# A recurrent-memory transformer on one core: the left rows' q and k of all segments made at once in step 0, against phase by phase in the steps

## The chip, the cores and the metric

The kernel runs on one core of one Trainium2 chip. The time is device time in microseconds (us) of one execution; what counts is the median over runs. The engines are PE (TensorE: PE for matmuls, PEld for its weight loads), DVE (VectorE), ACT (ScalarE), POOL (GpSimd) and SP (SyncE, which here only issues transfers). Transfers are moved by 16 DMA engines, whoever issues them.

## The reference

Two independent parts read the normalised input and are summed with it.

```
x = A_x                                   # [1, 2048, 1024], bf16
xn = layernorm(x)
out = x + A(xn) + B(xn)

A: mem = mem0                             # [8, 1024]
   for s in 64 segments of 32 rows:
       h = [mem ; xn of the segment]      # 40 rows
       q, k, v = h @ Wq, h @ Wk, h @ Wv   # 32 heads of 128, each W is 1024 x 4096
       p = softmax(mask(q k^T / sqrt(128)))   # memory rows see all rows; the others those up to their own
       o = (p v) @ Wo                     # 4096 x 1024
       mem = first 8 rows of o            # goes into the next segment
       out rows of the segment = the other 32

B: r = xn @ w_r; the two rows with the largest r go through a gated MLP (1024 -> 3584 -> 1024)
   and are added back, weighted by sigmoid(r)
```

The memory makes the 64 segments a chain: a segment can't begin before the one ahead has given its eight memory rows. Only what does not hang on the memory can be made ahead.

## The kernel before

**Steps.** One step is one segment. Its 40 rows are split: 32 "main" rows, the eight of memory and the first 24 of the segment, must be multiplied in the step. The last eight rows of the segment, the "left" rows, don't see the chain in their q, k and v; those of four segments are gathered to another block of 32 rows (a group G of four steps, j = 0 to 3 in it) and are multiplied one group ahead, in spare places of the steps.

**Weights.** Wq, Wk, Wv and Wo are 32 MB, cut in 64 granules of 512 KB, used in the same order in every step. 44 stay in SBUF after step 0 ("resident", tiles `wres`). 20 are "streamed": granule 6 is kept whole in PSUM (`KEPT`) and half of granule 25 too; the other 18.5 are fetched anew in every step from a packed copy in DRAM (`wsc`) into five slots (`wstream`, tiles `g`). `fetch` (L327) is issued by SP as soon as PE is done with the slot that is to be overwritten.

**A step.** It has six phases, `PHASES`, q and k of the first 16 heads, q and k of the others, then v in two halves. A phase p runs over eight granules, index kc: `PSm += ST[:, kc]^T W` (L669), four matmuls of 32 output rows side by side, with the 32 main rows as the stationary operand (`ST`) and 512 columns of weights moving. In phases where left rows are due, the same granule is used a second time with the left rows' `STL` (`left_pass`, L647). `left_of(s)` says which: in step j = 1 both q phases and in j = 2 both k phases for the next group, in j = 3 and j = 0 one v phase each; in step 0 all six for group 0. Between granules stand `hooks[p, kc]`: turning q and k (L516), scores (L534, L536), softmax, attention (L584, L586). Then 16 Wo granules, index w, add to `WO` (L730; the left rows' `WL` once in a group). The result's memory rows are written to `XN` (L791), whose end marks the end of a step, and turned into the next step's `ST`.

**Left q and k.** A left phase's PSUM (`PSl`) is copied to `XBl` (L695) and stored to DRAM in `ql_d` (L698), rows of a group by head columns. Each step loads its segment's share to `LX` (`new_lx`, L458, by POOL at w = 9 of the step before), turns it with four transposes at phase 1 kc 5 (`turn_lx`, L465) and copies it to `QKL` (L467), which scores read.

**Step 0** also loads the residents, x (`XP`, in the homes of late Wo granules, for the rows' statistics and B's router), makes the copies `wsc` (`copy_block`, 20 transfers by POOL), and spreads DVE's work over granules (`side`: statistics of 15 further tiles, `spread`, 16 `router_tile`). After step 63 the MLP of B follows, with its 22 MB of weights loaded into the homes that the last step leaves.

**Order.** The order on each engine and queue is written out by hand (`tc.manual_schedule()`): what is issued earlier in the program stands earlier in its engine's queue; semaphores for tiles' readers and writers are added to it.

Of the kernel before, what the change touches and what calls it, by code (L numbers as in the profile page):

```python
# [27 lines left out]
def kernel(  # L28
# [58 lines left out]

    def granule_out(t, g):
        return t[:, :] if g < 48 else t.rearrange("p (hh d) -> p hh d", hh=2)
# [14 lines left out]
    ql_d = [dram.tile([4, P, 512], BF16, name=f"ql_d{t}") for t in range(NT)]  # L104

# [14 lines left out]

    def load_resident(g):
        t = home(g, [P, 2048], BF16, f"wres{g}")
        nc.sync.dma_start(out=granule_out(t, g), in_=granule_dram(g))
        res_tiles[g] = t
# [52 lines left out]
    XP = {}  # L177

    def load_x(u):
        XP[u] = home(resident[-3 - u], [P, 2048], BF16, f"XP{u}")  # L180
        nc.sync.dma_start(out=XP[u].rearrange("p (a d) -> p a d", a=2),
                          in_=x2[2 * u * P:(2 * u + 2) * P, :].rearrange("(a p) d -> p a d", a=2))

    def xt(t):
        return XP[t // 2][:, (t % 2) * D:(t % 2 + 1) * D]

# [103 lines left out]
    def norm_left(t, G):  # L290
        mr = two_rows(ML[:, G, :], "ri")
        nc.vector.tensor_scalar(out=t[:, :], in0=t[:, :], scalar1=mr[:, 0:1], scalar2=mr[:, 1:2],
                                op0=ALU.subtract, op1=ALU.mult)

# [39 lines left out]
    def keep(g, t):  # L334
        for c, K in KEPT_COLS[g].items():
# [5 lines left out]
            nc.vector.tensor_copy(out=XK[:, :], in_=PTB)  # L341
# [29 lines left out]
    def fetch_moe():  # L371
        while moe and free_homes:
            what = moe.pop(0)
            h = free_homes.pop(0)
            t = home(h, [P, 2048], BF16, "MW") if h >= 0 else wstream.tile([P, 2048], BF16, tag="g", name="g")
# [16 lines left out]

    load_x(0)
    nc.sync.dma_start(out=WRB, in_=B_w_r.unsqueeze(0).to_broadcast([P, D]))
    load_seg(0)
    XL0 = load_left(0, one.tile([P, 256], BF16, tag="vl", name="XL0")[:, :])
# [4 lines left out]
    n_x = 1  # L401
    n_q = 0
    for g in range(48):
        if g in streamed:
            n_q += 1
            if n_q < N_SLOT:
                fetch()
            continue
        if n_q >= N_SLOT:
            break  # L410
        load_resident(g)
        if g % 2 == 1 and n_x < NT // 2:
            load_x(n_x)
            n_x += 1
    todo_res = [g for g in resident if g not in res_tiles]
# [6 lines left out]
    norm_left(XL0, 0)  # L422
    STL = new_stl(XL0)

    side = {}
    for t in range(1, NT):
        side[t] = lambda t=t: row_stats(xt(t), S6, MV[:, t, :])
    side[NT] = lambda: spread(1, NT)
    for t in range(NT):
        side[NT + 2 + t] = lambda t=t: router_tile(t)  # L430
    side[2 * NT + 2] = router_out
    side[2 * NT + 10] = router_top

    def after(s, g):

        if s == 0:
            if g in side:
                side[g]()
            if g % 2 == 1 and g >= 8 and to_copy:
                copy_block(to_copy.pop(0))  # L440
            if n_x_left and g % 2 == 1:
                load_x(n_x_left.pop(0))
            while todo_res and todo_res[0] <= g + 2 * 64 // n_str + 8 and (todo_res[0] < resident[-10] or g >= 2 * NT + 12):
                load_resident(todo_res.pop(0))
# [8 lines left out]
    n_x_left = list(range(n_x, NT // 2))  # L453

    def new_lx(s):
        t = lx[0] = one.tile([P, 512], BF16, tag="bA", name="LX")
        G, j = divmod(s, 4)
        nc.gpsimd.dma_start(out=t[:, :], in_=ql_d[G].rearrange("m (q s r) c -> (m q) s r c", q=4, s=4)[:, j])  # L458

    lx = [None]  # L460

    def turn_lx():
        PTq = PTB.rearrange("p (i c) -> p i c", i=4)
        for il in range(4):
# [463 lines left out]
```

## Time and profile before

| what | us |
|---|---|
| runs: median (lowest, highest) of 3 | 1919.79 (1911.71, 1925.86) |
| profiled execution: own time | 1914.95 |
| its span on the core | 1913.2 |
| end of step 0 (L791), end of step 63 | 129.9, 1852.2 |
| PE, DVE, ACT, POOL busy | 1607.9, 906.8, 703.0, 294.0 |

A row of a stretch of the span reads: start:end, length; busy us of PE, PEld, DVE, ACT and POOL with their instructions in brackets; the granted clock of PE (1.00 is full speed); the mean busy share of the 16 DMA engines; GB/s. A row of a group of instructions: line, engine, operation, out<-in, shapes, count | busy us, mean ns of one | idle time of the engine ahead of it and what ended that. A row of a wait: who waited (q: the engine's queue) <- for whom: us in all, times, longest. A row of transfers: out<-in, who issues, count, KB each, us from issue to landing. The mean of one matmul is its stay in the pipeline, some 380 ns; how fast they follow each other is read from busy time or from the chain, whose rows are start, us, what.

### The profile page before, as it was taken

The page shows a single profiled execution, that of the slowest core. Times are in us where ns is not written, and L with a number is a line of the kernel's source. Part 1 is how long each engine was busy: PE and PEld are TensorE (multiplying, and loading weights), DVE is VectorE, ACT ScalarE, POOL GpSimd, SP SyncE. Part 2 cuts the span into 40 slices and gives each one's busy share as a digit, 9 for nine tenths or more (in the row PEclk, how much of TensorE's full clock was granted, in tenths as well). Part 3 has the DMA queues.
Part 4 walks back from the last instruction along what each step waited for, and adds up shares of the span by engine and source line. Part 5 has one row for each costly group of instructions (what it writes and reads, how often), then busy time and mean ns, then how long its engine had stood idle before and what let it go on. Part 6 is the DMA issues. An engine that isn't in the chain of part 4 may idle for free. (4 is left out here: it accounts for less than half of the span.)

```text
span 1913.2 us, 82718 instructions
## 1 busy us (share of the span) xinstructions
PE 1607.9 (84%) x36320; PEld 891.0 (47%) x36320; DVE 906.8 (47%) x2884; ACT 703.0 (37%) x1886; POOL 294.0 (15%) x590
## 2 busy tenths in 40 slices
PE   3558898888889888989889898989888898889864
PEld 1224545444454445545454554545454544545443
DVE  6824544554455445444554454445444544455430
ACT  1113433443334343434344343334333443343320
POOL 2201111111110211112111111211121111111110
PEclk8669999999999999999999999999999999999995
DMA  9999999999999999999999999999999999999998
GB/s 369 399 363 378 358 381 365 380 379 354 383 352 390 350 382 376 378 381 369 387 353 373 370 372 362 362 387 365 370 363 384 376 366 385 365 386 368 393 390 330
DMA packets 224441, 712.39 MB, mean 372 GB/s; under 512 B 33664, under 2 KB 44464, under 8 KB 224080
## 3 DMA queue, kind: packets, MB, share of 16 engines
q1 hardware_dynamic: 194384, 671.18, 92.9%
q0 software_dynamic: 21056, 28.07, 4.4%
q10 hardware_dynamic: 8640, 7.87, 1.2%
q8 instruction: 283, 4.64, 0.9%
q14 instruction: 78, 0.64, 0.1%
HBM read 694.32 MB, written 22.29 MB: 375 GB/s over the span
## 5 line engine op out<-in xcount | busy, mean ns | idle before, releaser
L669 PE MATMUL PSm<-wres,ST 128*32 128x512 bf16 x8448 | 720.2, 385 | 21.2 <-DVE ST L283 6.7
L669 PEld LDWEIGHTS <-ST 128*32 128x32 bf16 x12288 | 325.8, 96 | 396.4 <-issue 166.9
L669 PE MATMUL PSm<-g,ST 128*32 128x512 bf16 x3588 | 362.4, 387 | 88.5 <-DMA g<-wsc 60.3
L685 ACT CAST XB<-PSm 128x512 bf16<-128x512 f32 x256 | 150.0, 586 | 306.9 <-PE PSm L669 305.3
L730 PEld LDWEIGHTS <-OT 128*32 128x32 bf16 x8192 | 214.1, 97 | 104.1 <-issue 80.8
L730 PE MATMUL WO<-wres,OT 128*32 128x256 bf16 x5632 | 237.2, 275 | 14.0 <-issue 8.9
L647 PE MATMUL PSl<-wres,STL 128*32 128x512 bf16 x2112 | 200.3, 390 | 1.5 <-issue 1.4
L526 DVE COPY KT<-BT 128x512 bf16<-128x512 bf16 x128 | 52.5, 410 | 307.7 <-ACT XB L685 148.9
L458 POOL DMA_DIRECT2D LX<-ql_d x63 | 33.8, 537 | 937.6 <-ACT OTL L593 525.0
L730 PE MATMUL WO<-g,OT 128*32 128x256 bf16 x2560 | 131.2, 279 | 54.4 <-DMA g<-wsc 42.0
L793 POOL DMA_DIRECT2D out_dram<-XN x256 | 129.6, 514 | 228.0 <-DVE XN L791 219.1
L707 ACT CAST VM<-PSm 128x512 bf16<-128x512 f32 x128 | 77.0, 602 | 153.5 <-PE PSm L669 121.5
L350 ACT COPY BK<-KEPT 128x512 bf16<-128x512 bf16 x126 | 78.3, 621 | 96.9 <-PE WO L730 96.9
L521 ACT COPY QT<-BT 128x512 bf16<-128x512 bf16 x128 | 75.0, 586 | 105.3 <-PE BT L516 99.7
L647 PEld LDWEIGHTS <-STL 128*32 128x32 bf16 x3072 | 85.1, 98 | 57.7 <-issue 8.0
L584 PEld LDWEIGHTS <-VM 32*128 32x128 bf16 x2048 | 67.6, 91 | 93.0 <-issue 71.3
L516 PEld LDWEIGHTS <-XB 128*128 128x128 bf16 x1024 | 58.5, 98 | 106.1 <-ACT XB L685 76.7
L543 DVE TENSOR_TENSOR BS<-BS,CT 128x96 f32<-128x96 f32 (+1 forms) x256 | 59.7, 233 | 100.8 <-PE BS L536 96.3
L354 DVE COPY g<-KEPT 128x512 bf16<-128x512 bf16 x126 | 47.6, 420 | 122.5 <-PE PSm L669 70.2
L791 DVE CAST XN<-WO 128x256 bf16<-128x256 f32 x64 | 27.2, 425 | 160.7 <-PE WO L730 160.7
L516 PE MATMUL BT<-IDENT,XB 128*128 128x128 bf16 x1024 | 102.0, 222 | 1.4 <-ACT QKL L476 1.4
L558 DVE TENSOR_REDUCE DN<-BS 128x8 f32<-128x320 f32 x128 | 63.0, 492 | 67.2 <-ACT BS L553 67.2
(168 smaller groups left out, 2382.2 us busy)
## 6 DMA issues: line engine op xcount, KB each, us to landing
g<-wsc SPq DMA_DIRECT2D x1134, 512.0 KB, 6.1
g<-wsc SPq DMA_DIRECT2D x63, 256.0 KB, 5.5
LX<-ql_d POOLq DMA_DIRECT2D x63, 128.0 KB, 6.0
ql_d<-XBl ACTq DMA_DIRECT2D x60, 128.0 KB, 5.6
MW<-in_B_w_gate_dram SPq DMA_DIRECT2D x16, 448.0 KB, 9.2
MW<-in_B_w_up_dram SPq DMA_DIRECT2D x16, 448.0 KB, 9.1
wres<-in_A_Wk_dram SPq DMA_DIRECT2D x12, 512.0 KB, 14.3
MW<-in_B_w_down_dram SPq DMA_DIRECT2D x12, 512.0 KB, 10.2
```

Of the source, the lines that this page charges most:

```text
L350: copy(out=back[c][:, :], in_=KEPT_COLS[KEPT_WHOLE][c])
L516: nc.tensor.transpose(out=PTq[:, il, :, :].rearrange("p j r -> p (j r)"), in_=XB[:, il * P:(il + 1) * P], identity=IDENT[:, :])
L521: nc.scalar.copy(out=QT[half][:, :, :], in_=pv)
L543: nc.vector.tensor_tensor(out=S4, in0=S4, in1=m, op=ALU.add)
L558: nc.vector.tensor_reduce(out=DN[:, :], in_=S8, axis=AX.X, op=ALU.add)
L584: nc.tensor.matmul(o, lhsT=VM[half][q0:q0 + 32, il * P:(il + 1) * P], rhs=PTm[q0:q0 + 32, il, 0:NK], start=True, stop=False, tile_position ...
L647: nc.tensor.matmul(PSl[32 * jq:32 * jq + 32, :], lhsT=STL[:, g % KC, :], rhs=part(Gv, jq), start=first_, stop=last_, tile_position=(0, 32 ...
L669: nc.tensor.matmul(PSm[32 * jq:32 * jq + 32, :], lhsT=ST[:, kc, :], rhs=part(Gv, jq), start=(kc == 0), stop=(kc == KC - 1), tile_position= ...
L685: nc.scalar.copy(out=XB[:, :], in_=PSm[:, :])
L707: nc.scalar.copy(out=VM[half][:, :], in_=PSm[:, :])
L730: nc.tensor.matmul(PS[32 * g:32 * g + 32, 0:256], lhsT=lhs(h), rhs=Gv[:, D * hs + 256 * g:D * hs + 256 * (g + 1)], start=False, stop=(last ...
L793: nc.gpsimd.dma_start(out=out2[s * SEG:s * SEG + XM, 256 * g:256 * (g + 1)], in_=OB[32 * g:32 * g + XM, :])
```

## The change

All 512 left rows of x (eight of each of 64 segments) are loaded at the start (`left_rows`), normalised (`left_stats`) and turned (`left_turns`) into `XLT`, 1024 x 512; its copy in DRAM, `xl_d`, serves the later groups' `STL`. In step 0, after each of the first four phases, `left_qk` multiplies the phase's eight granules with all left rows, now with the weights stationary: 16 heads x 8 granules of a 128 x 128 weight block against 512 moving columns. The products stand head by row at once, so that no turning is needed; they are gathered for half the heads in `GA` (4 MB, 64 segments) and stored to `ql_d` in 8 transfers per half, in pieces of 512 B. A step loads its `QKL` of 128 KB in one piece (`load_qkl`). The q and k left passes, `XBl`, `LX` and `turn_lx` leave the steps; v's left passes stay.

For the room, 18 resident granules share three areas (`AREAS`): `big0` holds the left rows and then the first half's `GA`, `big1` holds x and then the second half's, `pair` holds `XLT`. Their granules are loaded when that is done: `big0` after phase 1, `pair` after phase 3, `big1` in phase 5 of step 0. The `wsc` copies are issued ten each after phases 0 and 1; the other work of step 0 is placed after the phases.

```diff
+    AREAS = {"big0": [32, 34, 35, 37, 38, 40, 41, 43], "big1": [49, 51, 52, 54, 55, 57, 58, 60], "pair": [44, 46]}
...
-    ql_d = [dram.tile([4, P, 512], BF16, name=f"ql_d{t}") for t in range(NT)]
+    ql_d = [dram.tile([8, P, 512], BF16, name=f"ql_d{t}") for t in range(NSEG // 8)]
+    xl_d = dram.tile([NT, P, KC * SEG], BF16, name="xl_d")
...
+    def left_rows():
+        xs = x2.rearrange("(t s r) d -> t s r d", t=4, s=16)
+        for t in range(4):
+            nc.sync.dma_start(out=XLR[:, t, :], in_=xs[t, :, XM:SEG, :])
+
+    def left_stats():
+        for t in range(4):
+            row_stats(XLR[:, t, :], S6, MVL[:, t, :])
+        sd_rows(MVL, VEL)
...
+        for t in range(4):
+            nc.vector.tensor_scalar(out=XLR[:, t, :], in0=XLR[:, t, :], scalar1=RIL[:, t, 0:1], ...)
+
+    def left_turns():
+        for t in range(4):
+            PX = psA.tile([P, 1024], BF16, tag="acc", name="PX").rearrange("p (k t) -> p k t", k=KC)
+            for kc in range(KC):
+                nc.tensor.transpose(out=PX[:, kc, :], in_=XLR[:, t, kc * P:(kc + 1) * P], identity=IDENT[:, :])
+            (nc.scalar.copy if t % 2 else nc.vector.tensor_copy)(out=XLT[:, 4 * t:4 * t + 4, :, :]..., in_=PX...)
+        nc.scalar.dma_start(out=xl_d.rearrange("g p c -> p g c"), in_=XLT.rearrange("p g k r -> p g (k r)"))
...
-    def new_stl(t):
-        turn(t)
+    def new_stl(G):
         st = one.tile([P, KC, SEG], BF16, tag="stl", name="STL")
-        nc.scalar.copy(out=gview(st), in_=turned_x())
+        nc.gpsimd.dma_start(out=st.rearrange("p k r -> p (k r)"), in_=xl_d[G])
...
+    left_rows()
     load_x(0)
...
+    left_stats()
+    left_turns()
...
+    for t in range(1, NT):
+        row_stats(xt(t), S6, MV[:, t, :])
+    def left_qk(p, mat, half, Gs, between):
+        if mat == 0:
+            gathered[half] = area(f"big{half}", [P, NSEG, 256], "GA")
+        GA = gathered[half].rearrange("p s (m i q r) -> p s m i q r", m=2, i=4, q=4)
+        for h in range(16):
+            PSG = psA.tile([P, 512], F32, tag="acc", name="PSG")
+            for kc in range(KC):
+                nc.tensor.matmul(PSG[:, :], lhsT=Gs[kc][:, P * h:P * (h + 1)], rhs=XLT[:, :, kc, :],
+                                 start=(kc == 0), stop=(kc == KC - 1))
+            nc.scalar.copy(out=GA[:, :, mat, h % 4, h // 4, :], in_=PSG.rearrange("p (s r) -> p s r", r=XL))
+            if h % 2 == 1:
+                next(between, None)          # turning the kept granules, piece by piece
...
+        if mat == 1:
+            G3 = gathered[half]
...
+            for k in range(NSEG // 8):
+                nc.scalar.dma_start(out=ql_d[k][:, :, 256 * half:256 * (half + 1)].rearrange("s p c -> p s c"),
+                                    in_=G3[:, 8 * k:8 * (k + 1), :])
+        for g in range(8 * p, 8 * (p + 1)):
+            if g in streamed:
+                fetch()
+        if p == 0:
+            spread(1, NT)
+            for t in range(NT):
+                router_tile(t)
+            nc.gpsimd.tensor_copy(out=GATE, in_=gathered[0][:, 0, 0:4])
+        elif p == 1:
+            router_out()
+            area("big0", [P, 8, 2048], "W8A")
+            for g in AREAS["big0"] + [48]:
+                load_resident(g)
+        elif p == 2:
+            router_top()
+        else:
+            area("pair", [P, 2, 2048], "W2")
+            for g in AREAS["pair"]:
+                load_resident(g)
+        for _ in range((10, 10, 0, 0)[p]):
+            if to_copy:
+                copy_block(to_copy.pop(0))
 
     def after(s, g):
-        if s == 0:
-            if g in side:
-                side[g]()
...
+        if s == 0 and g == 41:
+            area("big1", [P, 8, 2048], "W8B")
+            for r in resident:
+                if r not in res_tiles:
+                    load_resident(r)
...
-    def new_lx(s):
-    def turn_lx():
-    def turn_first(mat, half, XBl):
...
+    def load_qkl(s):
+        t = qkl[0] = one.tile([P, 2, 2, 4, 4, XL], BF16, tag="bA", name="QKL")
+        nc.gpsimd.dma_start(out=t.rearrange("p h m i q r -> p (h m i q r)"), in_=ql_d[s // 8][s % 8])
...
     def left_of(s):
         G, j = divmod(s, 4)
         if s == 0:
-            return {ph: 0 for ph in PHASES}
+            return {(2, 0): 0, (2, 1): 0}
         if j == 0:
             return {(2, 1): G}
-        if G + 1 < NT:
-            return {(2, 0): G + 1} if j == 3 else {(j - 1, 0): G + 1, (j - 1, 1): G + 1}
-        return {}
+        return {(2, 0): G + 1} if j == 3 and G + 1 < NT else {}
...
-            hook(1, 5, turn_lx)
...
+            if j == 1 and p == 2 and G + 1 < NT:
+                STL = new_stl(G + 1)
...
-                    (nc.gpsimd if s == 0 else nc.scalar).dma_start(out=ql_d[left[mat, half]][2 * half + mat], in_=XBl)
...
+                if s == 0:
+                    left_qk(p, mat, half, [Gv_ for _, Gv_ in behind],
+                            (x for g_, Gv_ in behind if g_ in KEPT_COLS for x in keep(g_, Gv_)))
...
             if w == 9 and s + 1 < NSEG:
-                new_lx(s + 1)
+                load_qkl(s + 1)
```

More of the change, by code (lines that the diff above doesn't have):

```diff
@@ L86, in granule_dram, with area @@
         return Wo2[2 * w * P:(2 * w + 2) * P, :].rearrange("(hh e) d -> e hh d", hh=2)
+    AREAS = {"big0": [32, 34, 35, 37, 38, 40, 41, 43], "big1": [49, 51, 52, 54, 55, 57, 58, 60], "pair": [44, 46]}
+    place = {g: (tag, i) for tag, gs in AREAS.items() for i, g in enumerate(gs)}
+    areas = {}
+    def area(tag, shape, name):
+        areas[tag] = wres.tile(shape, BF16, name=name, tag=tag)
+        return areas[tag]
     def granule_out(t, g):
@@ L119, in home, with room @@
         return wres.tile(shape, dtype, name=name, tag=f"wres{g}")
+    def room(g, name):
+        if g not in place:
+            return home(g, [P, 2048], BF16, name)[:, :]
+        tag, i = place[g]
+        return areas[tag][:, i, :]
     def load_resident(g):
-        t = home(g, [P, 2048], BF16, f"wres{g}")
+        t = room(g, f"wres{g}")
         nc.sync.dma_start(out=granule_out(t, g), in_=granule_dram(g))
@@ L421 @@
     mem_to_st(OB, ST)
-    norm_left(XL0, 0)
-    STL = new_stl(XL0)
-    side = {}
+    left_stats()
+    left_turns()
+    STL = one.tile([P, KC, SEG], BF16, tag="stl", name="STL")
+    nc.vector.tensor_copy(out=STL[:, :, :], in_=XLT[:, 0, :, :])
     for t in range(1, NT):
[L427 to L432, printed above, removed]
@@ L481 @@
     group = {}
-    started = {}
     def left_out():
```

150 lines of the change are left out of this document (48 added, 102 removed).

## The prediction

> **What bounds the kernel now.** I read the page's slices and DMA queues first, then the stretches of the span, then the waits of PE and SP, then single steps.
>
> ```profile
> DMA  9999999999999999999999999999999999999998
> DMA packets 224441, 712.39 MB, mean 372 GB/s; under 512 B 33664, under 2 KB 44464, under 8 KB 224080
> q1 hardware_dynamic: 194384, 671.18, 92.9%
> q10 hardware_dynamic: 8640, 7.87, 1.2%
> ```
> ```profile
> 0.00:14.00 14.00, 1.29 (x11) 0.69 (x11) 6.92 (x38) 1.81 (x3) 5.46 (x20) 1.00 0.87 273
> 27.00:130.00 103.00, 48.11 (x643) 21.05 (x636) 60.07 (x130) 15.63 (x40) 16.34 (x29) 0.65 1.03 402
> 130.00:1000.00 870.00, 771.88 (x17640) 427.87 (x17644) 416.80 (x1351) 343.15 (x923) 136.39 (x271) 0.99 0.99 370
> ```
> ```profile
> SPq L327 <- PE PSm L669: 446.9, 593, 2.7
> SPq L327 <- DMA g<-wsc: 362.9, 680, 2.2
> ```
> ```profile
> PE PSm L669 <- DMA g<-wsc: 60.3, 125, 1.3
> PE WO L730 <- DMA g<-wsc: 42.0, 104, 1.2
> ```
> ```profile
> L791 DVE CAST XN<-WO x64: 424/425/426, 129.5 to 1851.7; 128x256 bf16<-128x256 f32 x64
> ```
>
> The DMA engines are busy in every slice. In step 0 (the first 130 us) they move 402 GB/s while PE is busy less than half of the time: step 0 is bound by loading. In the steps they are just as busy but move only 370 GB/s, and PE is busy 89%. SP's fetches wait for PE to free one of the five slots (447 us) about as much as for transfers (363 us), and PE waits 102 us for streamed granules. So a step is a loop of transfers and PE, nearly balanced: bytes count in full, PE's time only where it holds a slot back. L791 marks a step's end: (1851.7 - 129.5) / 63 = 27.3 us per step.
>
> **What the steps give back.** The change takes from 15 of the 16 groups the left rows' q and k passes (two phases in step j=1, two in j=2) with their evacuations and stores. Steps 61 and 62 of the kernel before already have this form: the last group has no successor, so it makes no left q and k and stores none. Against them I set the other j=1 and j=2 steps, cut at the ends of L791.
>
> ```profile
> 1775.00:1799.80 24.80, 20.85 (x476) 11.46 (x476) 12.04 (x39) 10.11 (x29) 3.28 (x7) 1.00 1.02 401
> 1799.80:1826.10 26.30, 21.38 (x476) 11.46 (x476) 12.29 (x41) 10.28 (x29) 3.25 (x7) 1.00 1.02 384
> ```
> ```profile
> 1338.30:1366.50 28.20, 24.34 (x539) 12.93 (x540) 12.52 (x41) 10.87 (x30) 3.28 (x7) 1.00 1.00 367
> ...
> sum 374.90, PE 337.38 PEld 180.73 DVE 175.96 ACT 152.20 POOL 45.91; mean PE 24.10 PEld 12.91 DVE 12.57 ACT 10.87 POOL 3.28
> ```
> ```profile
> sum 378.70, PE 332.42 PEld 176.04 DVE 180.49 ACT 152.60 POOL 45.39; mean PE 23.74 PEld 12.57 DVE 12.89 ACT 10.90 POOL 3.24
> ```
>
> The two sums are each over 14 windows: 26.8 us for j=1, 27.05 for j=2. Steps 61 and 62 take 51.1 together against 53.8, so 2.7 us less a group, for 5.6 us less PE: **-41 us** over 15 groups. Two steps are a small sample (one j=1 window has 28.2). The bounds: at least the stored bytes, 60 x 131 KB = 7.9 MB at 372 GB/s = -21; at most both steps at 24.8, -4.2 a group = -63.
>
> ```profile
> LX<-ql_d POOLq DMA_DIRECT2D x63, 128.0 KB, 6.0
> ql_d<-XBl ACTq DMA_DIRECT2D x60, 128.0 KB, 5.6
> ...
> OTL<-in_A_x_dram POOLq DMA_DIRECT2D x15, 64.0 KB, 6.0
> ```
>
> The step's LX load becomes a QKL load of the same size in the same place of POOL's queue, but it needs no turning.
>
> ```profile
> L465 PE MATMUL BT<-IDENT,LX 128*128 128x128 bf16 x252 | 24.3, 218 | 6.5 <-ACT QT L521 5.3 <-DMA LX<-ql_d 0.2
> L467 ACT COPY QKL<-BT 128x512 bf16<-128x512 bf16 x63 | 36.9, 586 | 35.9 <-PE BT L465 35.9
> ```
>
> Four transposes and the wait for QT go, (24.3 + 5.3) / 63 = 0.47 us of PE a step; ACT's copy ran beside PE's passes. It lies in phase 1, after which PE holds slots back, but transfers bound the rest of the step: 0 to -30 us, I take **-8**. The load was hidden before (0.2 us waited for it) and is now needed later, in phase 2; without that cover it would cost its 6 us per step. The left rows' loads for the later groups (15 x 64 KB) are replaced by 15 loads of turned rows of that size: 0. No instruction is added to a step, and no tag is asked for earlier than its last reader leaves it in PE's order, so I see no loss here.
>
> **What step 0 costs.** Its order: left rows loaded, normalised and turned ahead of PE's first pass; then four phases, each with 16 heads x 8 full 128x128 weights against 512 left rows.
>
> ```profile
> 4.65 1.28 DVE L190 BATCH_NORM_STATS2 MISC<-XP 128x6 f32<-128x512 bf16 x2 [0.21 <-DMA XP<-in_A_x_dram]
> 14.07 0.62 PE L669 MATMUL PSm<-wres,ST 128*32 128x512 bf16 x4
> ```
> ```profile
> L190 DVE BATCH_NORM_STATS2 MISC<-XP 128x6 f32<-128x512 bf16 x32 | 20.6, 685 | 8.7 <-DMA XP<-in_A_x_dram 8.3
> L191 DVE BATCH_NORM_AGGREGATE MISC<-MISC 128x2 bf16<-128x12 f32 x16 | 3.3, 209 | 0.6
> L217 DVE TENSOR_SCALAR XR<-XP,MISC 128x1024 bf16<-128x1024 bf16 x16 | 8.6, 537 | 0.4
> L219 DVE CUSTOM_DVE_ANT_0 XR<-XR,MISC 128x1024 bf16<-128x1024 bf16 x16 | 19.6, 1225 | 0.6
> L526 DVE COPY KT<-BT 128x512 bf16<-128x512 bf16 x128 | 52.5, 410 | 307.7 <-ACT XB L685 148.9 <-issue 81.9 <-ACT XBl L695 74.5
> ```
> ```profile
> 1698.28 0.43 PE PSm L669 x8
> 1698.71 0.33 PE BT L516 x4
> ```
>
> The first pass began at 14.1 us. Ahead of x now stand 1.05 MB, 2.6 us at 402 GB/s (partly under the wait for the other small loads). DVE then does four tiles' statistics (4 x 2 x 0.685 and 4 x 0.21: 6.3), four normalisations (4 x 0.54 = 2.1) and the last turned tile's copy (2 x 0.41): phase 0 begins at about **25**.
>
> Of the full product there is no row. 512 columns stream in 0.215 us (8 matmuls, four abreast, in 0.43); a 128-column turn with its own full weight load takes 0.33 / 4 = 0.083, of which 0.054 is streaming: at worst 0.029 of a load shows. So 512 matmuls cost 0.215 to 0.244 each, 110 to 125 us; weight loads overlap a longer stream, so I take 110. A phase is then 27.6 + 1.8 for the main pass. With 48 turns for the kept granules (4), 2 for a slow clock at the start and 4 for waits between phases (eight stores issued by ACT ahead of phase 2's copies are the nearest), phase 3 ends at 25 + 118 + 10 = **153**.
>
> The granted clock was 0.65 in the row of 27 to 130 us, where PE paused, and 0.99 where it was 89% busy; this product is dense, so I take 1. At 0.65 it would be 170 us. The Trainium skill, TensorE: Matmul & The Clock Gate, Part 1, says the same: half clock is the default, and some 3.4 us of sustained work releases it; by it nothing of the sum changes.
>
> DVE's work between (15 statistics, 16 router tiles of 1.76 us, 28 us in phase 1) lies beside PE's phases and just ends with them. Transfers pause in phases 2 and 3: the granules of the areas have no room.
>
> After 153 us these still have to move: the second half's stores, 4.2 MB, which must land before area big1 is loaded; 20 granules (two Wv, ten Wo, eight streamed), 10.5 MB at 402 GB/s = 26 us. The stores go in pieces of 512 B, of which there is no row. Queue 10 is the old stores in 1 KB pieces: 1.2% of 1913 = 23.0 us for 7.87 MB, against 20.8 at queue 1's 378 GB/s, so 2.2 us for 7680 extra pieces; with 16384 pieces both halves take 22.2 + 4.7 = 27, one half 13.5. Bounds: 11 at the full rate, 24.5 if a piece of 512 B costs as much as one of 1 KB. The Trainium skill, DMA: Bandwidth & Descriptors, Specifications, puts line rate at 512 B and more: by it the half takes 11.1 and the sum is 2.4 us lower. With 4 us from the last landing to the step's end: 153 + 13.5 + 26 + 4 = **197**, 67 us later than 130. The bounds of product, stores and start give +55 to +95. The first half's stores (half of 16, behind which area big0 loads) lie under phases 2 and 3; without that cover they would add 13.5.
>
> **The sum**, against the profiled execution's own 1914.95 (span 1913.2 and 1.75 around it; the median of the three runs, 1919.79, is 0.3% higher): 1914.95 + 67 - 41 - 8 = **1933**, 0.7% over the median.
>
> **Rivals.**
> 1. *Faster.* PE's release of slots, not bytes, bounds the steps: with the passes and the turning gone the fifth transfer is in flight sooner, both lightened steps fall to 24.8 and the turning counts in full: -63 - 30, 1915 + 67 - 93 = 1889. It decides once the steps give back more than step 0's 67 and 1% besides, 1.4 us a step. For it: step 61 at 401 GB/s; against: step 62, as light, at 384.
> 2. *Nothing to measure.* Step 0 ends early, at 185 (few waits, stores at the full rate): 1915 + 55 - 49 = 1921.
> 3. *Bytes alone.* The steps stay bound by transfers and only the stores' bytes come back: 1915 + 67 - 21 = 1961. For it: the DMA share, 1.00 to 1.02 in the j=1 and j=2 windows above; against: 370 GB/s where step 0 reached 402.
> 4. *A slow product.* Weight loads show, or the moving rows in runs of 64 B stream slower: +15 to +40, 1948 to 1973.
>
> That the passes don't leave the steps is no rival: PE's order is written out.
>
> **Chances.** Forecast 0.40, rivals 0.20, 0.13, 0.19, 0.08. The measurement tells about 1% (19 us) from no change, so slower means over 1938: rivals 3 and 4 and the upper half of the forecast's own spread (0.27 + 0.20), 0.47; faster, under 1901: rival 1, 0.20; the rest 0.33. The forecast alone spans 1913 to 1953; the range takes in rivals 1 to 3, 1888 to 1970.
>
> **What would show it.** Right: first L791 at about 197 us, PE dense at clock 1 from 30 to 150 with a DMA share well under 1 in phases 2 and 3, then a stretch of some 40 us at 400 GB/s with PE idle; steps of 26.5 us; 0.22 us per head matmul. Wrong: step 0 under 180 or over 215, steps under 26.0 or over 27.1, or PE waiting for QKL.

## The result: 3.3% slower

| kernel | median us | against before, 95% interval |
|---|---|---|
| before | 1920.79 | 1 |
| after | 1981.62 | 1.0331, 1.0287 to 1.0375 |

The profiled execution of after took 1995.09 us (span 1993.5), at the upper end of its runs, that of before 1914.95. Their difference is 80.1 us, where the medians differ by 61. The later comparisons are made by ratios to the kernel before, which ran beside each of them.

First the page of after, the lines that answer to those shown of before:

```profile
span 1993.5 us, 78747 instructions
...
DMA  9583999999999999999999999999999999999993
GB/s 349 222 285 96 339 384 381 399 370 394 361 394 361 375 384 388 385 378 370 356 400 359 382 361 395 362 387 354 381 384 384 388 379 389 366 397 375 399 405 111
DMA packets 234073, 714.15 MB, mean 358 GB/s; under 512 B 32192, under 2 KB 53744, under 8 KB 233728
...
q1 hardware_dynamic: 194960, 672.23, 88.3%
q0 software_dynamic: 20064, 27.45, 4.1%
q10 hardware_dynamic: 18704, 9.44, 1.6%
```

Before, every slice of the DMA row was a 9 but the last, an 8. Now the second, third and fourth slices and the last one are lower: transfers have holes in step 0 and behind the last step. In the slices of the steps the rate is 354 to 405 GB/s; about as many bytes as before are moved (714 MB against 712).

The ends of the steps, in the rows of the line that marks them:

```profile
L796 DVE CAST XN<-WO x64: 424/425/426, 235.4 to 1904.8; 128x256 bf16<-128x256 f32 x64
```

That cuts the difference of the spans, 80.3 us, into three parts. Step 0 ends at 235.8 us (the row's start and the 0.4 of the cast) instead of 129.9: **+105.9**. The 63 steps take 1904.8 - 235.4 = 1669.4 instead of 1722.2: **-52.8**, 26.50 us each. What lies behind the last step takes 88.3 instead of 61.1: **+27.2**. The prediction had +67, -49 and 0.

Step 0 of after by stretches (us, then busy time of each engine, the granted clock, DMA share, GB/s): phase 0; phase 1; a gap; phases 2 and 3; the end of the step.

```profile
27.80:60.00 32.20, 31.60 (x193) 15.08 (x193) 19.79 (x40) 12.95 (x22) 4.81 (x10) 1.00 0.90 317
60.00:96.70 36.70, 33.02 (x169) 14.07 (x168) 32.12 (x62) 10.77 (x20) 0.00 (x0) 0.91 0.56 221
96.70:125.50 28.80, 2.18 (x33) 0.98 (x34) 0.94 (x4) 0.03 (x1) 7.74 (x14) 0.61 1.02 327
125.50:187.60 62.10, 61.59 (x348) 27.56 (x351) 8.30 (x14) 22.78 (x39) 0.00 (x0) 0.96 0.31 110
187.60:235.80 48.20, 19.27 (x363) 9.79 (x362) 7.53 (x26) 6.85 (x22) 0.57 (x1) 0.65 1.01 341
```

In the third row PE, DVE and ACT stand for nearly all of the 29 us between phases 1 and 2; what POOL does there is mostly the issue of ten copies. What ACT and PE do there (the timeline of ACT, and the longest waits of PE over the run: total, times, longest):

```profile
96.14 0.59 ACT L474 CAST GA<-PSG 128x512 bf16<-128x512 f32 x1 [1.14 <-PE PSG L472]
96.76 28.66 ACTq L485 DMA_DIRECT2D ql_d<-GA  x8
125.52 0.30 ACT L570 COPY KT<-QKL 128x128 bf16<-128x128 bf16 x1 [28.79 <-DMA ql_d<-GA]
...
188.28 19.54 ACTq L485 DMA_DIRECT2D ql_d<-GA  x8
207.91 0.30 ACT L570 COPY KT<-QKL 128x128 bf16<-128x128 bf16 x1 [19.67 <-DMA ql_d<-GA]
```
```profile
PE PSm L697 <- DMA g<-wsc: 90.0, 194, 1.7
PE WL L745 <- DMA W8B<-in_B_w_down_dram: 44.6, 8, 40.0
PE BS L580 <- ACT KT L570: 43.6, 2, 26.6
PE WO L745 <- DMA g<-wsc: 43.4, 105, 1.8
PE BT L303 <- DVE XN L796: 25.4, 48, 0.5
```

ACT issues eight stores of gathered q and k, and the issue alone holds it for 28.66 us; the copy of k (L570) that the scores need is the next thing in its order, and PE waits 26.6 us for it. Phase 3's stores hold ACT for 19.5 us in the same way. The second row of the waits is another matter: PE stood 44.6 us in the left rows' pass over Wo (L745) for loads of the MoE part's down weights, which were sent into the same area (`W8B`). There was no such row before. In the order of time, SP's loads and the first matmuls of that pass:

```profile
1935.13 8.98 SPq L420 DMA_DIRECT2D W8B<-in_B_w_down_dram  x8
1944.92 0.65 PE L745 MATMUL WL<-W8B,OTL 128*32 128x256 bf16 x8 [39.98 <-DMA W8B<-in_B_w_down_dram]
```

PE's main pass over these eight granules was over by 1904. Then the down weights were loaded into their places, and only then did the left rows' pass read those places. So it didn't read Wo there: for the 32 left rows of the last group the changed kernel multiplies with down weights in place of eight of Wo's sixteen granules. The wait is the mark of a wrong order, not only of a late start. Before, that pass ran from 1851.5 to 1855.4, and the down weights were loaded from 1880 on.

The stretches behind the last step, of before, and of after:

```profile
1852.20:1870.00 17.80, 2.50 (x81) 2.25 (x80) 2.35 (x7) 2.98 (x4) 5.47 (x10) 0.74 1.03 405
1870.00:1890.00 20.00, 12.16 (x435) 11.88 (x433) 0.69 (x6) 1.65 (x3) 1.13 (x2) 0.50 1.03 400
1890.00:1913.00 23.00, 8.62 (x130) 3.73 (x129) 0.97 (x3) 0.22 (x1) 0.00 (x0) 0.50 0.69 256
```
```profile
1905.20:1920.00 14.80, 0.00 (x0) 0.00 (x0) 0.00 (x0) 0.00 (x0) 2.00 (x4) 0.63 1.03 409
1920.00:1940.00 20.00, 0.00 (x0) 0.00 (x0) 0.00 (x0) 0.00 (x0) 0.00 (x0) 0.50 1.03 405
1940.00:1960.00 20.00, 6.09 (x80) 3.32 (x79) 0.00 (x0) 0.37 (x1) 2.83 (x5) 0.50 0.80 293
1960.00:1980.00 20.00, 11.28 (x414) 11.19 (x415) 3.05 (x13) 4.26 (x5) 1.75 (x4) 0.50 0.15 52
1980.00:1993.50 13.50, 7.08 (x162) 4.83 (x158) 0.97 (x3) 0.22 (x1) 0.00 (x0) 0.63 0.01 2
```

Before, PE worked while the MoE weights came in. After, it is idle for 35 us, and all of the MoE matmuls come when the transfers are over.

### The profile page after: what moved, and what is told of

It is laid out like the page before. It is cut to its first block, busy times and chain, and to the rows that moved or that the text cites. A ratio compares the mean times of both kernels' runs of the same rounds, so it can differ in the third digit from the quotient of the medians.

```text
span 1993.5 us, 78747 instructions
## 1 busy us (share of the span) xinstructions
PE 1591.2 (80%) x34516; PEld 887.8 (45%) x34516; DVE 888.1 (45%) x2824; ACT 682.0 (34%) x1842; POOL 289.7 (15%) x586
## 3 DMA queue, kind: packets, MB, share of 16 engines
q1 hardware_dynamic: 194960, 672.23, 88.3%
q0 software_dynamic: 20064, 27.45, 4.1%
q10 hardware_dynamic: 18704, 9.44, 1.6%
## 5 line engine op out<-in xcount | busy, mean ns | idle before, releaser
L697 PE MATMUL PSm<-wres,ST 128*32 128x512 bf16 x5888 | 486.6, 384 | 18.4 <-DVE ST L327 16.9
L745 PEld LDWEIGHTS <-OT 128*32 128x32 bf16 x8192 | 217.6, 97 | 114.4 <-issue 91.1
L745 PE MATMUL WO<-W8B,OT 128*32 128x256 bf16 x4096 | 181.5, 277 | 10.2 <-issue 5.8
L745 PE MATMUL WO<-g,OT 128*32 128x256 bf16 x2560 | 133.5, 281 | 63.9 <-DMA g<-wsc 43.4
L527 POOL DMA_DIRECT2D QKL<-ql_d x63 | 36.3, 575 | 993.1 <-ACT OTL L639 368.5
L697 PE MATMUL PSm<-W8A,ST 128*32 128x512 bf16 x2048 | 180.1, 382 | 0.0
L472 PE MATMUL PSG<-XLT,wres 128*128 128x512 bf16 x368 | 104.7, 386 | 0.1
L745 PEld LDWEIGHTS <-OTL 128*32 128x32 bf16 x2048 | 72.7, 141 | 71.6 <-issue 58.4
L570 ACT COPY KT<-QKL 128x128 bf16<-128x128 bf16 x128 | 38.1, 298 | 183.4 <-PE BT L562 134.9
```

Source lines behind the costliest of these rows:

```text
L472: nc.tensor.matmul(PSG[:, :], lhsT=Gs[kc][:, P * h:P * (h + 1)], rhs=XLT[:, :, kc, :], start=(kc == 0), stop=(kc == KC - 1))
L697: nc.tensor.matmul(PSm[32 * jq:32 * jq + 32, :], lhsT=ST[:, kc, :], rhs=part(Gv, jq), start=(kc == 0), stop=(kc == KC - 1), tile_position= ...
L745: nc.tensor.matmul(PS[32 * g:32 * g + 32, 0:256], lhsT=lhs(h), rhs=Gv[:, D * hs + 256 * g:D * hs + 256 * (g + 1)], start=False, stop=(last ...
```

## Experiments

Three questions: what step 0 lost, what the tail lost, and from what the steps gained. Differences in us are differences of the ratios, times 1918; their 95% intervals are 8 to 15 us either way.

**The tail.** `after()` hands a granule's room to the MoE loads as soon as the main pass of step 63 is through with it, and the left rows' late pass over the same granules stands behind those loads in the program. The edit puts the loads behind the pass, so that the pass reads Wo again. The later versions with the stores on POOL have this edit too; all other runs keep after's tail, with what it multiplies there.

```diff
-            if g in resident:
+            if g in resident and g < 48:
                 free_homes.append(g)
 ...
+    free_homes += [g for g in resident if g >= 48]     # behind the last step's left passes
     free_homes += [-1] * N_SLOT
```

> The changed kernel, with one edit in its last step: the rooms of Wv and Wo granules (48 and up) are given to the MoE weights only after the step's late left-row pass over Wo, not in the middle of it. Theory: the 27 us that the tail grew by (88.3 against 61.0 us behind the last step) come from PE waiting in that pass for the MoE weights that were sent into the same room (44.6 us at L745), so the tail returns to 58 to 66 us and the kernel takes 1981.6 - 27 = 1955 (1950 to 1962). Rival: the tail is bound by the 8 MB of MoE weights or by the row loads behind it, which then only start later; the tail stays at 83 to 95 us and the time at 1975 to 1990. Step 0 (236 us) and the steps (26.5 us) stay as they are by both.

1953.61 us, ratio 1.018 (1.0147 to 1.0214), 29 us less than after.

```profile
1899.00:1915.00 16.00, 2.20 (x72) 1.71 (x64) 1.68 (x6) 0.53 (x2) 5.45 (x10) 0.75 1.03 405
1915.00:1935.00 20.00, 12.62 (x451) 12.40 (x452) 1.38 (x8) 4.10 (x5) 1.13 (x2) 0.50 1.03 401
1935.00:1958.00 23.00, 8.07 (x122) 3.50 (x118) 0.97 (x3) 0.22 (x1) 0.00 (x0) 0.50 0.74 274
```

The MoE matmuls (x451) again lie beside the transfers and the tail takes 60 us. The theory holds.

**Who issues the stores.** On top of that edit, ACT's two kinds of stores go to POOL:

```diff
-                nc.scalar.dma_start(out=ql_d[k][...
+                nc.gpsimd.dma_start(out=ql_d[k][...
 ...
-        nc.scalar.dma_start(out=xl_d...
+        nc.gpsimd.dma_start(out=xl_d...
```

> The edit of the tail, and the stores of the gathered q and k as well as that of the turned left rows issued by POOL instead of ACT. Theory: ACT stood for 28.7 us issuing eight stores of 512 KB in 512 B pieces, with the copies that PE waits for queued behind; on POOL nothing of PE waits there. Phase 2 then starts at about 100 us instead of 125.5, step 0 ends at 207 to 212 instead of 236, and the kernel takes 1925 to 1932. Rival: PE is held by the transfers themselves (the stores and ten copies of streamed granules at 331 GB/s), whoever issues them: the loads of the next phases wait behind the same bytes, step 0 ends at 230 or later, and the kernel takes 1950 or more. A second rival: POOL stands in turn, its copies of streamed granules and the loads of step 1 come late, and the gain turns up as waits of step 1 for QKL and XN.

1922.0 us, ratio 1.0026 (0.9999 to 1.0053): another 30 us, a little better than the theory's 1925 to 1932. The step ends, POOL's issues and two stretches (phases 0 to 3, the end of step 0):

```profile
L796 DVE CAST XN<-WO x64: 423/425/426, 200.1 to 1856.5; 128x256 bf16<-128x256 f32 x64
```
```profile
92.12 7.07 POOL L485 DMA_DIRECT2D ql_d<-GA  x8 [47.30 <-ACT GA L474]
...
154.73 7.08 POOL L485 DMA_DIRECT2D ql_d<-GA  x8 [31.80 <-ACT GA L474]
```
```profile
27.80:153.70 125.90, 123.65 (x739) 56.67 (x738) 61.11 (x119) 46.42 (x80) 20.90 (x33) 1.00 0.77 274
153.70:200.00 46.30, 20.22 (x363) 10.11 (x362) 7.15 (x25) 6.67 (x21) 7.65 (x9) 0.59 0.93 336
```

POOL issues eight stores in 7 us. PE is dense from 27.8 to 153.7, and step 0 ends at 200.5, better than the 207 to 212 expected. Neither rival shows. Both kinds of stores were moved at once, so their shares are not parted: the gap of 28.8 us is gone, and phases 0 to 3, without the gap, take 125.9 us instead of 131.0 (32.2 + 36.7 + 62.1).

**What makes the issue slow.** Two edits of after that leave the stores on ACT. One takes the ten copies away that run beside the first eight stores:

```diff
-        for _ in range((10, 10, 0, 0)[p]):
+        for _ in range((20, 0, 0, 0)[p]):
```

> The changed kernel with all twenty copies of streamed granules issued behind phase 0, none behind phase 1, so that fewer bytes compete with the first eight stores of gathered q and k. Theory: ACT stands 28.7 us because the queue takes only as many pieces as it has sent, so the issue goes as fast as the stores land; with the copies gone from that stretch its 8 stores of 512 KB need 10 to 14 us (4.2 MB at 331 to 400 GB/s), PE's stand of 25.5 us shrinks to 7 to 14, step 0 ends at 222 to 228 and the kernel takes 1967 to 1975. Rival: the issue costs its time by the number of pieces alone (8192 in 28.7 us, 3.5 ns each): ACT stands 26 to 29 us as before, step 0 ends at 232 to 238, and the time stays at 1976 to 1986.

The other makes a piece of a store 4 KB instead of 512 B:

```diff
-    ql_d = [dram.tile([8, P, 512], ...
+    ql_d = [dram.tile([2, P, 8, 256], ...
 ...
-                nc.scalar.dma_start(out=ql_d[k][:, :, 256 * half:256 * (half + 1)].rearrange("s p c -> p s c"),
+                nc.scalar.dma_start(out=ql_d[k][half],
```

> The changed kernel with the DRAM tensor of the gathered q and k laid out so that a store's piece is 4 KB (8 segments of one half for one partition) instead of 512 B; a step's load then takes two pieces of 512 B for each partition instead of one of 1 KB. ACT still issues the stores. Theory: ACT's stand is one of pieces (1024 a store): with 128 a store it issues all eight in 3 to 5 us, phase 2 starts at about 100 us, step 0 ends at 204 to 212 instead of 236, the steps lose 0 to 5 us by the load's smaller pieces, kernel 1950 to 1960. Rival: the issue goes as fast as bytes land whatever the pieces: ACT stands 15 to 29 us, step 0 ends at 225 to 238, kernel 1970 to 1990.

ACT's timeline in the first, then in the second:

```profile
106.31 12.48 ACTq L485 DMA_DIRECT2D ql_d<-GA  x8
118.89 0.30 ACT L570 COPY KT<-QKL 128x128 bf16<-128x128 bf16 x1 [12.61 <-DMA ql_d<-GA]
```
```profile
96.22 8.90 ACTq L485 DMA_DIRECT2D ql_d<-GA  x8
105.22 0.30 ACT L571 COPY KT<-QKL 128x128 bf16<-128x128 bf16 x1 [9.03 <-DMA ql_d<-GA]
...
167.69 13.46 ACTq L485 DMA_DIRECT2D ql_d<-GA  x8
```

Without copies beside them the same 8192 pieces were issued in 12.5 us instead of 28.7. So the number of pieces alone doesn't set the time; what else is in the queues does too. As a kernel it gained only 3 us (1977.39, ratio 1.0316), with 10 either way, which is less than expected: phase 1, with all twenty copies beside its loads, ended ten us later. That time lies in the rival's range, but the rival's reason, 26 to 29 us of standing as before, falls. With 4 KB pieces and the copies still there, ACT stood for 8.9 us, and 1958.17 us (ratio 1.0219, 21 less than after) is in the theory's range, though step 0 ended at 214 and not at 204 to 212: the stand is short, but not the 3 to 5 us of a cost by pieces. Both matter: the size of a piece, and what else is in the queues. The issue doesn't last until all has left: when it ended, ACT's queue had moved 3.25 MB of the 4.19 in after, 3.00 without the copies, and 1.72 with 4 KB pieces. So neither "as fast as the stores land" nor "by pieces" gives the time alone; how far an engine may run ahead was not tried. The smaller pieces of the step's load cost nothing that shows: the 63 steps took 1649 us, less than in any other run.

```profile
L797 DVE CAST XN<-WO x64: 424/425/426, 213.6 to 1862.7; 128x256 bf16<-128x256 f32 x64
```

The packet counts say why the size matters. In after, ACT's queue (q10 on the page above) moved 9.44 MB in 18704 packets, 505 B each. With the stores on POOL, the queues of the page are:

```profile
DMA packets 217945, 714.15 MB, mean 372 GB/s; under 512 B 32192, under 2 KB 35312, under 8 KB 217600
q1 hardware_dynamic: 194960, 672.23, 91.2%
q0 software_dynamic: 22640, 36.89, 5.7%
```

The 9.44 MB came to q0 with 22640 - 20064 = 2576 packets: 3.7 KB each from the same pieces. The Trainium skill, DMA: Bandwidth & Descriptors, Queues, rings and completion order, says that a DMA engine goes round its queues packet by packet. By it, a queue of 505 B packets gets a small share beside one of large packets. Stretches of the trace agree: from 112 to 116 us of after ACT's queue sent 358 packets and POOL's, with the copies, 354, but 0.18 MB against 1.30; with 4 KB pieces, from 110 to 115 us, 284 and 284, 1.04 MB against 1.03. 28.7, 12.5 and 8.9 us fit this; no run changed the size of packets and nothing else.

**From what the steps gained.** Three runs put one part back into the steps. They leave step 0 and the tail as in after, and nothing reads what they add.

The stores alone (two of 128 KB in j = 1 and j = 2, on ACT):

```diff
+        if s > 0 and j in (1, 2) and G + 1 < NT:
+            def store_again():
+                nc.scalar.dma_start(out=sc_d[n_sc[0] % 8][:, :], in_=res_tiles[0][:, 0:512])
+                n_sc[0] += 1
+            hook(j, 0, store_again)
+            hook(5, 7, store_again)
```

> The changed kernel with two stores of 128 KB given back to each step j = 1 and j = 2 (groups 0 to 14), into DRAM that nobody reads; no passes, no copies. It measures the bytes' share of what the steps gained (1722.3 to 1669.3, 53 us). By the third rival of the prediction (bytes alone) the 60 stores, 7.9 MB, bring back all of what j = 1 and 2 gained: +21 at 372 GB/s, the steps then take 1688 to 1692 us together and the kernel 2000 to 2005. By the theory that PE's release of slots gave the gain the stores lie under PE's time: steps 1669 to 1677, kernel 1980 to 1989.

The passes alone, straight behind the main pass:

```diff
+            if s > 0 and j in (1, 2) and G + 1 < NT and mat == j - 1:
+                PSd = psL.tile([P, 512], F32, tag="accl", name="PSd")
 ...
+                        if PSd is not None:
+                            for jq in range(4):
+                                nc.tensor.matmul(PSd[32 * jq:32 * jq + 32, :], lhsT=ST[:, g_ % KC, :], rhs=part(Gv_, jq), ...
```

> The changed kernel with the left rows' q and k passes put back into the steps j = 1 and j = 2 as matmuls alone (two phases each, the same weights, the step's own rows as stationary side, into a PSUM tile that nobody reads); no evacuation, no store. It measures PE's share of what the steps gained. Over four kernels with the changed steps they took 1656 to 1669 us together (mean 1662) against 1722 before, and the two stores a step put back gave +20. Theory: the passes count for the rest, because PE's time in a step sets when slots come free: +20 to +40, kernel 2002 to 2022. By the third rival of the prediction (bytes alone) the passes lie beside transfers: +0 to +6, kernel 1979 to 1989.

The turning alone:

```diff
+                for il in range(4):
+                    nc.tensor.transpose(out=PTq[:, il, :], in_=res_tiles[0][:, il * P:(il + 1) * P], identity=IDENT[:, :])
+                ts = one.tile([P, 512], BF16, tag="bC", name="TS")
+                nc.scalar.copy(out=ts[:, :], in_=PTB)
+            hook(1, 5, turned_again)
```

> The changed kernel with the turning put back into each step but the first: four transposes of 128x128 and an ACT copy of 128x512 in phase 1, on a resident granule, into a tile that nobody reads. The prediction put its removal at -8, bounds 0 and -30. Theory: PE's 0.33 us a step lies beside transfers for the most part: +3 to +10, kernel 1983 to 1993. Rival: it counts in full with the wait for it, 0.47 us a step: +30, kernel 2006 to 2014.

The passes in line came out above the theory's 40 us, and above all that the steps had gained. (The next text calls that as much as PE's added time allows; 15 groups of 5.8 us would be 87.) What that run lacked was the order of the kernel before, so it was made again with the old places:

```diff
+                later = [g for g in rest if g in res_tiles] if half == 1 else []
+                for at, g in zip(((4, 3), (4, 4), (4, 5), (5, 0), (5, 0), (5, 2), (5, 2)), later):
+                    hook(*at, lambda g=g, ...: pass_again(PSd, ST, g, res_tiles[g], False, l_))
 ...
+            gs = [g for g in resident if g // 8 == pf][:4]           # behind the last step's Wo, as in before
+            fill = [lambda g=g, PSn=PSn: pass_again(PSn, STL, g, res_tiles[g], g == gs[0], False) for g in gs]
```

> Again the changed kernel with the left rows' q and k passes put back into the steps j = 1 and j = 2 as matmuls alone, now at the places at which the kernel before had them: up to four resident granules' passes at the end of the step before, where PE waits for the state, the second half's resident granules in phases 4 and 5, the main passes ahead of them at a phase's start. The run with all passes straight behind the main pass took 2045.0 us, 63 more than the changed kernel and as much as PE's added time (5.8 us a group) allows at most. Theory: in their old places a good part of them filled PE's waits and held no slot back: +25 to +40 only, kernel 2006 to 2022. Rival: PE's time counts in full wherever the passes stand: +55 to +68, kernel 2036 to 2050.

And all three at once, the passes at their old places:

> The passes at their old places, the two stores of 128 KB a step and the turning, all three put back into the changed kernel (without the left rows' evacuations). Alone the stores cost +20, the turning +18. Theory: together they bring back what the steps gained, 1722 against a mean of 1662 us, +50 to +65, kernel 2032 to 2047, less than the sum of the three alone, since bytes and PE's time lie partly beside each other. Rival: they add up, +75 to +100, kernel 2057 to 2082.

| put back | median us | ratio, 95% interval | us over after | 63 steps in the profile, us |
|---|---|---|---|---|
| nothing (after) | 1981.62 | 1.0331 (1.0287 to 1.0375) | 0 | 1669.4 |
| stores | 2001.93 | 1.0435 (1.0406 to 1.0463) | 20 | 1683.5 |
| passes, in line | 2045.03 | 1.0667 (1.061 to 1.0725) | 64 | 1717.7 |
| turning | 1999.58 | 1.0398 (1.0336 to 1.0461) | 13 | 1682.9 |
| passes, old places | 1997.09 | 1.0426 (1.039 to 1.0462) | 18 | 1670.3 |
| all three | 2037.77 | 1.0614 (1.0576 to 1.0653) | 54 | 1721.5 |

The last column is last minus first start of the marking row, which for the last two runs reads:

```profile
L826 DVE CAST XN<-WO x64: 424/425/426, 233.4 to 1903.7; 128x256 bf16<-128x256 f32 x64
```
```profile
L842 DVE CAST XN<-WO x64: 424/425/426, 233.5 to 1955.0; 128x256 bf16<-128x256 f32 x64
```

All three bring the steps back to the 1722 of before, so within the noise the gain is accounted for, though the left rows' evacuations are left out. Whether the parts overlap, as the theory had it, can't be told: 20, 18 and 13 make 51, and together they cost 54, 11 either way. (The text above takes 18 for the turning, the difference of the medians; by the ratios it is 13.) The stores cost 20, 10 either way, which fits all their bytes (21 was reckoned at 372 GB/s). The passes cost 18 in their old places, 11 either way, and 64 in line, 14 either way; in the profiled execution with the old places the steps took no longer than in after, so its size is uncertain, but the difference of the two is clear. Both expectations for the in-line run's size and the theory's 25 to 40 for the old places were off, and the rival that PE's time counts wherever it stands falls. The kernel before had put passes where PE waited. The turning lies between its two expectations, and its interval, some 15 us either way, doesn't tell 8, 18 or nearly nothing apart.

**A version that beats both.** The stores on POOL and the mended tail reach the time of before. What is left in step 0 is the stretch behind phase 3, bound by transfers (153.7 to 200). So q and k are gathered in two rooms of four granules in turn, each stored as soon as its phase is through, and half of `big1` is loaded under phase 3:

```diff
-    XP = area("big1", ...            # and the left rows in big0
+    XP = area("big0", ...            # and the left rows in big1
 ...
-            gathered[half] = area(f"big{half}", [P, NSEG, 256], "GA")
+        G3 = gathered[0][:, 4 * mat:4 * mat + 4, :].rearrange("p a d -> p (a d)").rearrange("p (s c) -> p s c", c=128)
 ...
+            c0 = 256 * half + 128 * mat
+            nc.gpsimd.dma_start(out=ql_d[k][:, :, c0:c0 + 128].rearrange("s p c -> p s c"), ...
 ...
             router_top()
+            for g in AREAS["big1"][0:4]:
+                load_resident(g)
```

> The kernel with the tail mended and the stores on POOL (1922 us, step 0 ended at 200), and with q and k gathered in two rooms of four granules each (both in area big1, in turn q and k) instead of two areas of eight: each phase's quarter is stored as soon as it is made, in pieces of 256 B; x stands in big0 and the left rows in big1; four of big1's granules of Wo are loaded under phase 3, and after phase 3 only 2.1 MB are left to store and four granules fewer to load. Theory: the end of step 0 is bound by bytes behind phase 3 (4.2 MB of stores and 10.5 MB of granules, 44 us of it); 4.2 MB fewer are 10 to 12 us, and step 0 ends at 186 to 190, kernel 1908 to 1913. Rival: pieces of 256 B land so slowly, or POOL stands so long at 32 stores, that what is saved is lost: step 0 ends at 197 to 206, kernel 1918 to 1930.

1911.16 us, ratio 0.996 (0.9928 to 0.9991), in the theory's range, and step 0 ended at 186.3. Then the left rows' statistics and turning go ahead of the first tile's:

```diff
+    left_stats()
+    left_turns()
     row_stats(xt(0), S6, MV[:, 0, :])
 ...
-    left_stats()
-    left_turns()
```

> The kernel with two rooms of four granules (1911 us, 0.4% under before), with the left rows' statistics and turning issued ahead of the first tile's, since they land first: DVE stood idle until 9.4 us, while the left rows were there. Theory: the first main pass starts at 23 to 25 us instead of 28, phases 0 to 3 are dense from there on, so step 0 ends 3 to 5 us earlier, at 181 to 184, kernel 1906 to 1909. Rival: the x tiles then come later behind DVE and PE waits for them behind phase 0, or step 0's end is bound by transfers: no change, 1909 to 1914.

**1902.75 us, ratio 0.9921 (0.989 to 0.9952)**: 0.8% under before, a small difference whose interval leaves out 1. Step 0 ended at 182.9, in the expected range; the kernel is below the expected 1906 to 1909, but the 7.5 us that this edit brought have 8.5 either way. Its step ends, and step 0 by stretches (start, phases 0 to 3, end):

```profile
L797 DVE CAST XN<-WO x64: 424/425/428, 182.5 to 1844.6; 128x256 bf16<-128x256 f32 x64
```
```profile
0.00:24.50 24.50, 7.52 (x69) 4.91 (x73) 17.28 (x59) 4.04 (x6) 5.92 (x20) 1.00 0.91 326
24.50:151.00 126.50, 123.91 (x750) 56.79 (x742) 60.32 (x119) 46.03 (x80) 35.26 (x49) 1.00 0.91 319
151.00:183.00 32.00, 17.96 (x335) 9.75 (x332) 7.34 (x25) 6.55 (x21) 6.85 (x9) 0.63 1.01 368
```

PE starts at 24.5 and stays dense until phase 3 is through; the end takes 32 us instead of 46. Step 0 costs 53 us more than before (183 against 129.9), the steps give 60 back (1722.2 - 1662.1).

## Why the prediction was wrong

The forecast was 1933, its range 1888 to 1970. The profiled execution took 62 us more than the forecast: step 0 39 more, the tail 27 more, the steps 4 less. Two terms failed, both on the side of loss.

- **"4 for waits between phases (eight stores issued by ACT ahead of phase 2's copies are the nearest)"** is the term that failed most. It named the place, but costed the issue as next to nothing. It took 28.7 us, and PE stood for 26.6 of them. The cover named for the first half's stores ("lie under phases 2 and 3") wasn't there: not the bytes were in the way but the engine that issued them, with phase 2's copies behind. Moved to POOL, the stores did lie under phases 2 and 3. The 13.5 us reckoned without that cover would have been half of it. The second half's issue, 19.5 us, cost little: behind phase 3 step 0 took 48.2 us with it and 46.8 without. Step 0 over 215 us was one of the named signs of being wrong; it ended at 235.8.
- **The tail** had no term at all. In the program, step 63's late passes stand behind the fetches of the MoE weights into the same area. That cost 29 us in the runs. Before, each granule's place was a tile of its own, and the load of the next tile in it stands behind all readers of the old one, the late pass too (in after SP still waits 10.3 us for that pass with a down granule that has such a place). The change made eight places one tile with one name: there the pass, which stands later, is taken for a reader of the load's data, and waits for it and reads it. The trace of before could not show that; the order of `after()` and `fill` in the code could have.

One reading was wrong as well, and the forecast didn't rest on it. "SP's fetches wait for PE (447 us) about as much as for transfers (363 us)" takes one row of several: the same view has 194.8 us for the left passes, 136.8 and 67.1 for Wo's and smaller ones, 926 in all. So fetches waited for PE two and a half times as long as for transfers, and "nearly balanced" doesn't follow from these waits. In after the sums are 814 and 418. The forecast of the steps came from steps 61 and 62; what the misreading bore on is the weight of rival 1 against rival 3.

With both losses mended, the sum comes out, and most of its terms:

- Step 0: forecast 197, measured 200.5. Phase 0 began at 27.8, not 25; phases 0 to 3 ended at 153.7, where 153 was reckoned; behind them 46.8, where 43.5 was (13.5 + 26 + 4). Its parts are not the reckoned ones: the loads into `big1` began at 179.0, 25 us behind phase 3 and not 13.5, while five other granules had been issued meanwhile.
- The price of small pieces: 27 us for the 8.4 MB of both halves. In after ACT's queue took 1.6% of the span, 32 us, for 9.44 MB of such pieces, some 28 for 8.4; at queue 1's rate it would be 22.
- The product: as forecast. In the timeline of after, three matmuls take 0.65 us from start to start, 0.216 each (bounds 0.215 to 0.244), so the weights' loads don't show, and rival 4 falls. The clock was 0.91 to 1.00 in the dense stretches.

```profile
74.79 0.81 PE L472 MATMUL PSG<-XLT,wres 128*128 128x512 bf16 x3
75.44 0.38 PE L472 MATMUL PSG<-XLT,g 128*128 128x512 bf16 x1
```

- Transfers in phases 2 and 3: in after the share fell to 0.31; with both mended, with stores, copies and `big0`'s granules there, it was 0.79 from 92 us on. Behind phase 3 transfers ran at 341 GB/s in after and 336 with both mended, not 400, and PE was not idle there but had 19 to 20 us of work.
- The steps: -49 forecast, -53 in the profiled execution, and 26.50 us a step, the number given. Over six kernels whose steps are those of after (after, the runs of tail, POOL, copies, rooms and order) the 63 steps took 1656 to 1669, on average 1662, so -60 is the better figure. By parts: the prediction took its -41 whole; with 21 for the bytes, its own lower bound, 20 are left for PE, and put back they cost 20 and 18. The turning, -8, measured 13. All three with the intervals above.
- PE has no wait for the steps' loads of `QKL`, of which the prediction had named one as a sign of being wrong.
- Rival 3 (bytes alone, 1961) is nearest in time, but its reason is wrong: the steps gave all that the forecast had. Rival 1's 93 us from the steps did not come. Rival 2, step 0 early, did not come either, though with both losses mended the time, 1922, is that of rival 2.

So the sizes reckoned for bytes and PE held. What was missed is who issues, what stands behind in that engine's order, and what a later reader of a place still needs.

## What to carry to other kernels

A store with many small pieces can hold its issuing engine for much of the time in which the queue moves it: put it on an engine with nothing urgent behind it, or make the pieces larger. When work is moved to another place in a buffer's life, read all the code that loads into that buffer next, also at the end of the program, and ask who still reads it: a new wait for a load with which a pass has nothing to do can mean that the pass reads that load's data. And work that fills waits can cost a fraction of what it costs in line (18 against 64 us here), so moving it away gives back only that fraction.

## What the runs showed of the hardware

- Eight stores of 512 KB in 512 B pieces held ACT for 28.7 us beside ten copies of 512 KB and for 12.5 us without them; in 4 KB pieces for 8.9 us with them. POOL issued the same stores in 7.07 us.
- From the same pieces, ACT's queue made packets of 505 B and POOL's of 3.7 KB.
- In stretches in which both were at work, ACT's and POOL's queues sent about equal numbers of packets of very different size: 358 and 354 in 4 us of after, with 0.18 and 1.30 MB; with 4 KB pieces 284 and 284 in 5 us, with 1.04 and 1.03 MB.
- 128 x 128 weights against 512 moving columns ran at 0.216 us a matmul, with no weight load to be seen between them.

Not the chip's doing is another wait in after, of a load that SP issued, for a store of ACT with no data in common:

```profile
SPq L200 <- DMA xl_d<-XLT: 26.4, 1, 26.4
```

This is SP's wait ahead of a load of x, for the turned left rows' store. In the program as it is built, the transfers of SP and ACT use eight completion semaphores in turn, and each waits until the one ahead on its semaphore has landed; this load follows that store on the same one. POOL's transfers use others, and in the run with the stores on POOL the wait was gone.
